# Output products of the late attention heads queued on TensorE behind a feed-forward product

## The chip, the cores and the metric

One core of a Trainium2 chip runs the whole program. The metric is the device time of one execution in microseconds (us). The kernel before was timed three times: 1084.61, 1088.86 and 1091.10 us, median 1088.86 us.

## The reference

```python
# q, k, v: (4, 8, 576, 64), f: (4, 8, 576); 32 heads in all, D = 64
scores = q @ k.T / sqrt(D);  cum = cumsum(log(clip(f, 1e-4, 1)))
scores = where(causal, -1e9, scores + cum[i] - cum[j])
attn   = softmax(scores);    attn_out = attn @ v
x = attn_out as (2304 tokens, 512)          # 4 batches x 576 tokens, 8 heads x 64
h = relu(x @ w1_in);   x = (h * h) @ w1_out          # first feed-forward, d_ff = 2048
h = x @ w2_in;         out = (h - tanh(h)) @ w2_out  # second feed-forward, d_ff = 2048
```

## The kernel before

All three parts run in one stream. Feed-forward operands are kept as a high and a low float32r part, and each product is the sum of three matmuls (high by high, low by high, high by low).

**Feed-forward.** The loop at the end of the kernel runs over steps g. Sixteen steps make a block of tokens (j, i = divmod(g, 16)). Blocks 0 to 7 are the first feed-forward, with 288 tokens each (block j needs the attention of batch j // 2). Blocks 8 to 12 are the second one. Step g calls `h_step` (L131), a product of 12 matmuls into the tile `hp`, then Relu and two Squares on ScalarE, which give `gh`, and a subtraction, which gives `gl` (on VectorE, except for the first two blocks). Two steps later (LAG = 2) `y_step` (L158) adds 12 matmuls into the tiles `yp`, 8 of them from `gh` and 4 from `gl`. `gh` and `gl` have three buffers each, and `hp` has one PSUM bank until block 6. Below, h 67 and y 67 are the products of step g = 67; the count starts at 0, so that 68 steps are done once y 67 is.

**Attention.** It runs beside blocks 0 to 5 as a generator, `chain()`, which hands out 196 pieces; `advance(to)` (L655) draws pieces up to a number given by `PACE`. It is called twice in a step, behind `h_step` and behind `y_step`. Pieces 116 to 195 are those of the late heads: five for each k from 17 to 32 (`attention_late`, L580). In the five pieces the scores of head k are made (`s_ps`, 12 matmuls), softened, turned by VectorE into the tile T (`turn`), and written to DRAM from T by one DMA (`put`, 1 MB), while the head before, k - 1, is finished: `split_p` splits its attention tile PTl into PTh (four instructions of POOL, L90) and a new PTl (four of VectorE, L101), and `pv` (L493) makes the output product, ten matmuls, of which those at L518 read PTh and PTl. Behind the fifth piece `get(k)` reads head k back from DRAM into PTl by four DMAs. PTl, PTh and T have one buffer each. So `get(k)` has to wait for `put(k)` and for `pv(k - 1)`, and `pv(k)` has to wait for `get(k)` and the split. With an odd head `pv` is followed by `store_x`, which writes a pair of heads to `x_d`; block 6 starts with a load of `x_d` (L705), which needs the last pair, heads 30 and 31.

**Order of the work.** Every engine runs its instructions in the order of its queue. For what is emitted before block 2 that order is the order of emission. Behind it a planner picks the order of each engine by its own simulated times. It is free to put `pv` ahead of feed-forward products that were emitted earlier, when by its times PTh and PTl are there. One rule limits it from the other side: `h_step` is queued behind the last TensorE instruction of an attention piece some pieces back (`SLK`: 8 in block 1, 3 in block 2, 8 in blocks 3 and 4, no rule in block 5).

By `PACE` the output products of heads 16 to 31 are emitted right behind these feed-forward products (head: product): 16: y 31; 17: y 34; 18: y 37; 19: y 40; 20: h 45; 21: y 49; 22: h 55; 23: y 56; 24: y 62; 25: y 67; 26: h 74; 27: h 79; 28: y 80; 29: y 83; 30: y 86; 31: y 89. For head 25, as an example: its `pv` lies in piece 116 + 5 x 9 + 4 = 165; in block 4 the pieces go from 160 to 177 over 32 half steps, and 160 + int(17 x 12 / 32) = 166 is reached in the second call of i = 5, that is in step 69, behind y 67.

Of the kernel before, what the change touches and what calls it, by code (L numbers as in the profile page):

```python
# [53 lines left out]
def kernel(  # L54
# [10 lines left out]
    nc = tc.nc  # L65
# [14 lines left out]
    def pre(u):  # L80
        return "" if u < UT else "l_"

    def by(name):
        return {"A": nc.scalar, "V": nc.vector, "P": nc.gpsimd, "S": nc.sync}[ENG[name]]

    def rounded(eng, out, in_):
        if eng is nc.scalar:
            eng.activation(out, in_, AF.Copy)  # L88
        elif eng is nc.gpsimd:
            eng.tensor_scalar(out, in_, 1.0, 1.0, ALU.mult, ALU.mult)  # L90
        else:
            eng.tensor_copy(out, in_)
# [114 lines left out]
    def load(u):  # L207
        R[u] = one.tile([128, 2, S], F32, tag="R", name="R")
        nc.sync.dma_start(R[u], qk[u])
        QB[u] = two.tile([68, 2, S], F32R, tag="QB", name="QB")  # L210
        nc.sync.dma_start(QB[u][64:68].bitcast(F32), aug_d[u])
# [7 lines left out]
    def prep(u):  # L219
        r = R.pop(u)  # L220
        qa = two.tile([128, 2, S], F32R, tag="QA", name="QA")
        QA[u] = qa
        split_qk(r, qa, QB[u], *(pre(u) + x for x in ("qb_q", "qa_lo", "qb_lo")))
        ST[u] = two.tile([128, 4, 6], F32, tag="ST", name="ST")
        by(pre(u) + "st").memset(ST[u], 1.0)

    def load_v(u):
        VR[u] = two.tile([128, 5, D], F32, tag="VR", bufs=2, name="VR")
        nc.sync.dma_start(VR[u], v[u])

    def prep_v(u):
        VH[u] = one.tile([128, 4, 2, D], F32R, tag="VH", name="VH")
        rounded(by(pre(u) + "vh"), VH[u][:, :, 0], VR[u][:, 0:4])
        rest(by(pre(u) + "vl"), VH[u][:, :, 1], VR[u][:, 0:4], VH[u][:, :, 0])
# [167 lines left out]
    def store_x(b, pair, xs, c0, c1):  # L402
        STORED.add((b, pair, c1))
        n = c1 - c0
        xh = one.tile([128, S], F32R, tag="xsh", name="xsh")
        rounded(by(pre(b * H) + "xh"), xh[:, :n], xs[:, c0:c1])
        rest(by(pre(b * H) + "xl"), xs[:, c0:c1], xs[:, c0:c1], xh[:, :n])
        nc.sync.dma_start(x_d[b][pair][:, 0, c0:c1], xh[:, :n].bitcast(F32))
        nc.sync.dma_start(x_d[b][pair][:, 1, c0:c1], xs[:, c0:c1])
# [21 lines left out]
    def bank(u, name):  # L431
        return psa.tile([128, 512], F32, tag="at", name=name)

    def scores(u, t):
        qa, qb, st = QA[u], QB[u], ST[u]
        n, q0 = NKEY[t], Q0[t]
        rows = 64 if t == 0 else 128
        cuts = [(0, 320), (320, 576)] if t == 4 else [(0, n)]
        mn = None
        for i, (a, b) in enumerate(cuts):  # L440
            ps = bank(u, "s_ps")
            nc.tensor.matmul(ps[:, :b - a], qa[:, 0, q0:q0 + 128], qa[:, 1, a:b], start=True, stop=False)  # L442
            nc.tensor.matmul(ps[:, :b - a], qb[:, 0, q0:q0 + 128], qb[:, 1, a:b], start=False, stop=True)  # L443
            mn = row_min(P[t], ps, st, t, i, a, b, mn)
        soften(P[t], st, t, mn, f"{pre(u)}n{t}")
# [20 lines left out]
    def turn(t):  # L466
        p, T = P[t], PT["t"]
        if t == 0:
            nc.vector.transpose(T[0:64, 0:2, 3, 0], p[0:64, :64].rearrange("p (b j) -> p b j", b=2))
            return  # L470
        nch = min(t + 1, 4)
        nc.vector.transpose(T[:, :, :nch, t - 1].rearrange("p b a j -> p a b j"),  # L472
                            p[:, :nch * 128].rearrange("p (a b j) -> p a b j", a=nch, b=4))
        if t == 4:
            nc.vector.transpose(T[:, 0:2, 2, 0], p[:, 512:576].rearrange("p (b j) -> p b j", b=2))

    def put(u):
        by("put").dma_start(p_d[u % 2], PT["t"].rearrange("p b a s j -> p (b a s j)"))
# [7 lines left out]
    def split_p(a):  # L486
        hi, lo = PT["h"], PT["l"]
        for c in (2 * a, 2 * a + 1):
            s0 = max(0, c - 1)
            rounded(by("pth"), hi[:, :, c, s0:], lo[:, :, c, s0:].bitcast(F32))  # L490
            rest(by(f"ptl{c}"), lo[:, :, c, s0:], lo[:, :, c, s0:].bitcast(F32), hi[:, :, c, s0:])

    def pv(u):  # L493
        vh, vr = VH.pop(u), VR.pop(u)
        b, h = divmod(u, H)
        e = h % 2
        ps = bank(u, "o_ps")
        if u < UT:
            hi, lo = (PT[k].rearrange("p q a s j -> p (q a s j)").rearrange("p (c t j) -> p c t j", c=4, t=4) for k in "hl")
            po = ps.rearrange("p (s j) -> p s j", s=4)  # L500
            at = lambda p, c, t: p[:, c, t:]
            po4, p4 = ps[0:64, 384:512].rearrange("p (q j) -> p q j", q=4), PT["t"][0:64, :, 3, 1]
            po_at = lambda t: po[:, t:]
            p0 = PT["t"][0:64, 2:4, 3, 0]
        else:
            hi, lo = PT["h"], PT["l"]
            po = ps.rearrange("p (q s j) -> p q s j", q=4, s=4)
            at = lambda p, c, t: p[:, :, c, t:]
            po4, p4 = po[0:64, :, 3], lo[0:64, :, 2, 0].bitcast(F32)
            po_at = lambda t: po[:, :, t:]  # L510
            p0 = lo[0:64, 0:2, 3, 0].bitcast(F32)
        seq = [(hi, 0), (hi, 1), (lo, 1), (hi, 2), (lo, 2), (hi, 3), (lo, 3), (None, 4), (lo, 0)]
        for n, (pt, c) in enumerate(seq):
            if pt is None:
                nc.tensor.matmul(po4, vr[0:64, 4], p4, start=False, stop=False)  # L515
                continue
            t = max(0, c - 1)
            nc.tensor.matmul(po_at(t), vh[:, c].rearrange("p a d -> p (a d)"), at(pt, c, t), start=(n == 0), stop=(n == 8))  # L518
        ps0 = bank(u, "o0_ps")
        nc.tensor.matmul(ps0[0:64, 0:64], vr[0:64, 0], p0, start=True, stop=True)  # L520
        if e == 0:
            XS[0] = two.tile([128, S], F32, tag="xs", name="xs")
        xs = XS[0]
        r = slice(64 * e, 64 * e + 64)
        xt = one.tile([64, 512], F32, tag="xsh", name="xt")
        rounded(nc.scalar, xt, ps[64:128])
        if u < UT:
            nc.vector.tensor_tensor(xs[r, 64:], ps[0:64], xt, ALU.add)
        else:
            nc.vector.tensor_tensor(  # L530
                xs[r, 64:].rearrange("p (s q j) -> p q s j", s=4, q=4),
                ps[0:64].rearrange("p (q s j) -> p q s j", q=4, s=4),
                xt.rearrange("p (q s j) -> p q s j", q=4, s=4), ALU.add,
            )
        rounded(by(pre(u) + "xs0"), xs[r, 0:64], ps0[0:64, 0:64])
        if e == 1:
            store_x(b, h // 2, xs, 0, S)
# [42 lines left out]
    def attention_late():  # L580
        for k in range(UT + 1, NU + 1):
            now = k < NU
            if now:
                load_v(k)
                scores(k, 4)
            yield
            if now:
                scores(k, 3)
                turn(4)
            yield  # L590
            if k + 1 < NU:
                prep(k + 1)
            prep_v(k - 1)
            split_p(0)
            if now:
                scores(k, 2)
                turn(3)
            yield
            if k + 2 < NU:
                load(k + 2)  # L600
            split_p(1)
            if now:
                scores(k, 1)
                scores(k, 0)
                turn(2)
            yield
            if now:
                turn(1)
                turn(0)
                put(k)  # L610
            pv(k - 1)
            yield
            if now:
                get(k)
# [26 lines left out]
    def chain():  # L641
        yield from first_b()
        steady_init()
        load(H)
        yield from attention(H)
        yield from attention_late()

    ga = chain()
    cnt = [0]
    PEI = {}  # L650
    NB_PIECES = 5 * H
# [1 line left out]
    total = A1 + 5 * (NU - UT)  # L653

    def advance(to):  # L655
        while cnt[0] < min(to, total):
            next(ga, None)
            PEI[cnt[0]] = next(x for x in reversed(nc.cur_bb.bb.instructions) if x.engine == EngineType.PE)
            cnt[0] += 1
# [78 lines left out]
    for g in range(len(BLK) * NF + LAG):  # L738
# [40 lines left out]
        if j < len(PACE):  # L779
            lo, hi, end = PACE[j]  # L780
            advance(lo + int((hi - lo) * min(1.0, (2 * i + 2) / end)))
# [60 lines left out]
```

## Time and profile before

| What | Value |
|---|---|
| Time of the profiled execution / its span | 1085.49 us / 1083.6 us |
| Median of three timed runs | 1088.86 us |
| TensorE matmul busy | 1026.8 us, 95% |
| TensorE weight load busy | 897.2 us, 83% |
| VectorE / ScalarE / GpSimd busy | 596.5 / 524.8 / 248.4 us |
| Mean granted TensorE clock | 0.987 |
| Chain that ended last | TensorE 58%, DMA 9%, VectorE 4% |

The span starts with attention and weight preparation. The late heads run from about 270 to 560 us beside blocks 2 to 5, the rest of the first feed-forward follows until about 675 us, and the second feed-forward fills the rest. In the profile PE is TensorE, PEld its weight loads, DVE is VectorE, ACT is ScalarE, POOL is GpSimd, and SP is the engine whose queue issues all DMAs here. PEclk is the granted clock as a share of 2.4 GHz; the trace knows two levels, 2.4 and 1.2 GHz.

### The profile page before, as it was taken

The numbers are of one execution on the slowest core, as the hardware profiler recorded it, in microseconds if no ns is written. First come the engines' busy times: TensorE is split into PE (matmuls) and PEld (weight loads), VectorE is DVE, ScalarE is ACT, GpSimd is POOL, SyncE is SP. The second block draws the span as 40 slices with busy tenths as digits, with TensorE's granted clock in tenths as the row PEclk, the third lists the DMA queues.
The fourth block names the chain that finished last, engine by engine and source line by source line (L and its number), as shares of the span: only waits on it lengthen the run. The fifth ranks groups of instructions, "written<-read, shape, count | busy, mean of one in ns | idle before, by whom it ended". The sixth has DMA issues, their size and how long they took to land.

```text
span 1083.6 us, 16842 instructions
## 1 busy us (share of the span) xinstructions
PE 1026.8 (95%) x6048; PEld 897.2 (83%) x6048; DVE 596.5 (55%) x1599; ACT 524.8 (48%) x1221; POOL 248.4 (23%) x357
## 2 busy tenths in 40 slices
PE   3889999999999898999989999999999999999998
PEld 3577678888998788988989999888888888888898
DVE  7897767777787777877524546542222222222232
ACT  5987777765555546454526657432222222222232
POOL 4243455564453442533210000000000000000000
PEclk9999999999999999999989999999999999999999
DMA  6565643225955648845546088100200300110010
GB/s 207 222 167 179 196 145 120 90 84 172 294 170 179 205 146 259 257 141 162 169 148 253 2 281 306 45 1 8 109 1 1 117 1 1 39 39 1 1 40 21
DMA packets 63301, 134.83 MB, mean 124 GB/s; under 512 B 6416, under 2 KB 31568, under 8 KB 61168
## 3 DMA queue, kind: packets, MB, share of 16 engines
q1 hardware_dynamic: 63216, 133.74, 38.7%
q8 instruction: 48, 0.79, 0.3%
q14 instruction: 37, 0.30, 0.1%
HBM read 93.94 MB, written 39.78 MB: 123 GB/s over the span
## 4 chain that ended last, share of the span: by engine, by line
PE 58%; DMA 9%; DVE 4%; POOL 1%; SPq 1%; ACT 1%; issue 1%; POOLq 0%; DVEq 0%
PE yp L164 28%; PE hp L138 27%; DMA PTl<-p_d 6%; DMA p_d<-T 3%; PE o_ps L518 2%; DVE PTl L101 2%; SPq L484 1%; POOL PTh L90 1%; DVE gl L101 1%; DVE T L472 1%; DVE QA L101 0%; PE s_ps L442 0%; PE s_ps L443 0%; PE o_ps L515 0%; ACT P L425 0%
## 5 line engine op out<-in xcount | busy, mean ns | idle before, releaser
L138 PE MATMUL hp<-xhl,w 128*128 128x288 f32 (+2 forms) x2496 | 451.4, 328 | 3.9 <-ACT tmp L148 2.2
L138 PEld LDWEIGHTS hp<-xhl,w 128*128 128x128 f32 x2496 | 386.0, 190 | 42.4 <-ACT tmp L148 3.7
L164 PE MATMUL yp<-ghl,w 128*128 128x512 f32 (+1 forms) x960 | 216.0, 374 | 0.0
L164 PE MATMUL yp<-gh,w 128*128 128x288 f32 x1024 | 200.3, 301 | 0.1
L164 PEld LDWEIGHTS yp<-ghl,w 128*128 128x128 f32 x960 | 168.4, 188 | 34.5
L153 DVE TENSOR_TENSOR tmp<-hp,tmp 128x512 f32<-128x512 f32 (+1 forms) x80 | 51.0, 638 | 209.9 <-ACT tmp L152 209.9
L164 PEld LDWEIGHTS yp<-gh,w 128*128 128x128 f32 x1024 | 162.0, 192 | 2.6 <-issue 1.1
L152 ACT ACTIVATE tmp<-hp 128x512 f32<-128x512 f32 (+1 forms) x80 | 44.4, 555 | 225.0 <-PE hp L138 224.9
L164 PE MATMUL yp<-gl,w 128*128 128x288 f32 x512 | 135.2, 303 | 3.6 <-DVE gl L101 2.8
L148 ACT ACTIVATE tmp<-hp 128x288 f32<-128x288 f32 x128 | 51.8, 406 | 115.2 <-PE hp L138 112.1
L425 ACT ACTIVATE P<-P,ST 128x320 f32<-128x320 f32 (+4 forms) x151 | 84.6, 562 | 38.5 <-DVE ST L416 38.1
L164 PEld LDWEIGHTS yp<-gl,w 128*128 128x128 f32 x512 | 91.3, 192 | 6.4 <-DVE gl L101 3.9
L101 DVE TENSOR_TENSOR ghl<-tmp,ghl 128x512 fp32r<-128x512 f32 (+1 forms) x80 | 51.1, 638 | 49.1 <-ACT ghl L88 49.1
L429 POOL TENSOR_SCALAR P<-P,ST 128x448 f32<-128x448 f32 (+4 forms) x88 | 55.9, 636 | 96.3 <-DVE ST L428 53.7
L416 DVE CUSTOM_DVE_ANT_0 P<-s_ps,mk 128x320 f32<-128x320 f32 (+3 forms) x151 | 63.8, 432 | 21.7 <-PE s_ps L443 14.4
L101 DVE TENSOR_TENSOR gl<-tmp,gh 128x288 fp32r<-128x288 f32 x96 | 47.7, 498 | 49.7 <-ACT tmp L150 49.2
L88 ACT ACTIVATE ghl<-tmp 128x512 fp32r<-128x512 f32 (+1 forms) x80 | 47.2, 590 | 49.9 <-DVE tmp L153 49.8
L101 DVE TENSOR_TENSOR PTl<-PTl,PTh 128x512 fp32r<-128x512 f32 (+1 forms) x64 | 51.9, 840 | 35.2 <-POOL PTh L90 35.1
L101 DVE TENSOR_TENSOR w<-wst,w 128x512 fp32r<-128x512 f32 x64 | 45.6, 719 | 28.1 <-ACT w L88 28.0
L90 POOL TENSOR_SCALAR PTh<-PTl 128x512 fp32r<-128x512 f32 (+1 forms) x64 | 46.4, 750 | 56.9 <-DMA PTl<-p_d 56.3
L149 ACT ACTIVATE gh<-tmp 128x288 fp32r<-128x288 f32 x128 | 56.5, 443 | 4.1 <-PE yp L164 1.2
L150 ACT ACTIVATE tmp<-tmp 128x288 f32<-128x288 f32 x128 | 56.1, 439 | 2.2
(120 smaller groups left out, 1194.6 us busy)
## 6 DMA issues: line engine op xcount, KB each, us to landing
raw<-in_w_dram SPq DMA_DIRECT2D x64, 512.0 KB
p_d<-T SPq DMA_DIRECT2D x16, 1024.0 KB
PTl<-p_d SPq DMA_DIRECT2D x64, 256.0 KB
R<-in_qk_dram SPq DMA_DIRECT2D x24, 576.0 KB
xhl<-y_d SPq DMA_DIRECT2D x16, 512.0 KB
xhl<-x_d SPq DMA_DIRECT2D x14, 576.0 KB
y_d<-yst SPq DMA_DIRECT2D x14, 576.0 KB
VR<-in_v_dram SPq DMA_DIRECT2D x32, 160.0 KB
```

The lines of the kernel that those rows point to most:

```text
L88: eng.activation(out, in_, AF.Copy)
L90: eng.tensor_scalar(out, in_, 1.0, 1.0, ALU.mult, ALU.mult)
L101: eng.tensor_tensor(out, in_, hi.bitcast(F32), ALU.subtract)
L138: nc.tensor.matmul(ps, w[:, k * 128:(k + 1) * 128], xk, start=(jj == 0), stop=(jj == 11))
L148: nc.scalar.activation(tmp, ps, AF.Relu)
L149: nc.scalar.activation(gh, tmp, AF.Square)
L150: nc.scalar.activation(tmp, tmp, AF.Square)
L153: nc.vector.tensor_tensor(tmp, ps, tmp, ALU.subtract)
L164: nc.tensor.matmul(yp[m][:, :n], w[:, c], x, start=(i == 0 and j == 0), stop=(i == NF - 1 and j == 2))
L416: nc.vector.tensor_tensor_reduce(p[:rows, a:b], ps[:rows, :b - a], mk[:rows, o:o + b - a], -0.125, 3.0e38 if mn is None else mn, ALU.add, ...
L425: nc.scalar.activation(p[:rows, :n], p[:rows, :n], AF.Exp, bias=mn, scale=-1.0, accum_out=st[:rows, 1, t:t + 1])
L429: by(n_by).tensor_scalar(p[:rows, :n], p[:rows, :n], st[:rows, 3, t:t + 1], 1.0, ALU.mult, ALU.mult)
```

## The change

`advance` notes the TensorE instruction that was emitted last before it draws pieces, which is the last matmul of an `h_step` or a `y_step`, in `FF[0]`. In `attention_late` the call of `pv(k - 1)` is wrapped in `tc.issue_after(FF[0])`: each TensorE instruction that `pv` emits gets an edge that puts it behind that matmul in TensorE's queue. The edge is on the order of the queue alone; there is no semaphore and no wait for the matmul to end. What `pv` puts on the other engines has no such edge. The planner plans again with these edges.

```diff
@@ attention_late @@
                 turn(1)
                 turn(0)
                 put(k)
-            pv(k - 1)
+            with tc.issue_after(FF[0]):
+                pv(k - 1)
             yield
             if now:
                 get(k)
@@
     ga = chain()
+    FF = [None]
     cnt = [0]
     PEI = {}
@@
     def advance(to):
+        FF[0] = next(x for x in reversed(nc.cur_bb.bb.instructions) if x.engine == EngineType.PE)
         while cnt[0] < min(to, total):
             next(ga, None)
```

## Rows read from the trace of the kernel before

**Rows 1.** The page, busy time, share of the span, instructions:
```profile
PE 1026.8 (95%) x6048; PEld 897.2 (83%) x6048; DVE 596.5 (55%) x1599; ACT 524.8 (48%) x1221; POOL 248.4 (23%) x357
```

**Rows 2.** Waits of TensorE, 270 to 560 us: total us, times, longest:
```profile
PE o_ps L518 <- POOL PTh L90: 15.5, 8, 4.2
PE yp L164 <- DVE gl L101: 2.8, 2, 1.5
```

**Rows 3.** Sums by stretch, feed-forward alone: busy us (instructions) by engine, PEclk, DMA, GB/s:
```profile
560.00:675.00 115.00, 115.00 (x862) 114.78 (x861) 56.40 (x112) 72.77 (x164) 0.00 (x0) 1.00 0.62 220
```

**Rows 4.** Timeline of TensorE, first product of heads 21, 25, 27, 29, 31:
```profile
358.34 0.50 PE L518 MATMUL o_ps<-PTh,VH 128*128 128x512 f32 x1 [3.59 <-POOL PTh L90]
...
433.91 0.50 PE L518 MATMUL o_ps<-PTh,VH 128*128 128x512 f32 x1 [1.58 <-POOL PTh L90]
...
471.79 0.49 PE L518 MATMUL o_ps<-PTh,VH 128*128 128x512 f32 x1 [1.10 <-POOL PTh L90]
...
509.55 0.69 PE L518 MATMUL o_ps<-PTh,VH 128*128 128x512 f32 x1 [1.85 <-POOL PTh L90]
...
546.09 0.80 PE L518 MATMUL o_ps<-PTh,VH 128*128 128x512 f32 x1 [4.21 <-POOL PTh L90]
```

**Rows 5.** Sums by stretch around three of these products:
```profile
430.00:440.00 10.00, 8.42 (x49) 7.77 (x49) 8.59 (x21) 4.38 (x13) 5.73 (x6) 0.83 0.77 220
505.00:515.00 10.00, 8.15 (x47) 7.33 (x47) 7.71 (x27) 3.58 (x13) 3.76 (x6) 0.83 0.59 168
546.00:552.00 6.00, 5.91 (x26) 5.24 (x27) 3.68 (x7) 1.30 (x3) 2.33 (x4) 0.61 0.01 3
```

**Rows 6.** L164 (y products) up to the first product of heads 21, 25, 27, 29, 31:
```profile
0.00:358.33 358.33, 96.28 (x585) 84.11 (x585) 0.99 0.56 173
...
0.00:433.90 433.90, 126.63 (x772) 111.59 (x772) 0.98 0.57 177
...
0.00:471.78 471.78, 143.40 (x876) 126.89 (x876) 0.98 0.58 180
...
0.00:509.54 509.54, 156.48 (x964) 139.06 (x964) 0.98 0.58 180
...
0.00:546.08 546.08, 171.11 (x1056) 152.46 (x1056) 0.98 0.58 178
```

**Rows 7.** L138 (h products) up to the first product of heads 27 and 31:
```profile
0.00:471.78 471.78, 141.75 (x888) 126.78 (x888) 0.98 0.58 180
...
0.00:546.08 546.08, 168.69 (x1068) 151.84 (x1068) 0.98 0.58 178
```

**Rows 8.** Timeline around head 21, ScalarE, then VectorE:
```profile
353.75 0.43 ACT L150 ACTIVATE tmp<-tmp 128x288 f32<-128x288 f32 x1
...
358.32 1.09 DVE L101 TENSOR_TENSOR PTl<-PTl,PTh 128x512 fp32r<-128x512 f32 x1 [4.86 <-POOL PTh L90]
...
362.02 0.91 DVE L101 TENSOR_TENSOR gl<-tmp,gh 128x288 fp32r<-128x288 f32 x1
```

**Rows 9.** Timeline of TensorE, last product of heads 27, 28, 29, 31:
```profile
477.85 0.50 PE L518 MATMUL o_ps<-PTl,VH 128*128 128x512 f32 x1
...
500.47 0.50 PE L518 MATMUL o_ps<-PTl,VH 128*128 128x512 f32 x1
...
517.32 0.50 PE L518 MATMUL o_ps<-PTl,VH 128*128 128x512 f32 x1
...
553.53 0.50 PE L518 MATMUL o_ps<-PTl,VH 128*128 128x512 f32 x1
```

**Rows 10.** Timeline of SP: put and get of head 28, load of block 6:
```profile
480.67 0.33 SPq L478 DMA_DIRECT2D p_d<-T  x1
...
485.67 1.75 SPq L484 DMA_DIRECT2D PTl<-p_d  x4
...
558.25 1.95 SPq L705 DMA_DIRECT2D xhl<-x_d  x2
```

**Rows 11.** Timeline of TensorE, h 95 and the start of block 6:
```profile
568.24 3.76 PE L138 MATMUL hp<-xhl,w 128*128 128x288 f32 x27
```

## The prediction

> **What bounds the kernel now.** I read the page first: TensorE holds a matmul for 95% of the span [rows 1], so the end is moved only by what lets TensorE stand still or slows it. The waits of TensorE in the stretch of the late heads come second. One line carries most of them: the first output product of a head, which waits for PTh from POOL, 15.5 us in eight waits; the y products wait for `gl` 2.8 us in two [rows 2]. The sums by stretch come third. With feed-forward alone TensorE is never idle, and 862 matmuls take 115.0 us [rows 3], 133.4 ns each, 1.60 us for a product of twelve; I price every h and y product with that. The timeline comes fourth: heads 21, 25, 27, 29 and 31 begin with an idle TensorE, 3.59, 1.58, 1.10, 1.85 and 4.21 us [rows 4], 12.3 of the 15.5 us. What the reader is to see: TensorE has work left (feed-forward), and it stands behind an instruction that isn't ready. PTh needs a round trip through DRAM, and the planner's order expects it sooner than it comes.
>
> There is a second cost. Behind the waits of heads 25, 29 and 31 the granted clock falls to 0.83, 0.83 and 0.61 of the stretch [rows 5]. With two levels, 2.4 and 1.2 GHz, the work lost is (1 - 0.83) x 10 = 1.7 us, again 1.7, and (1 - 0.61) x 6 = 2.3, in sum 5.7 us. Without the wait I expect no fall: with TensorE kept busy it is granted in full [rows 3].
>
> **Which heads move.** The edge matters only where `pv` now runs ahead of its named product. The matmuls counted up to the first product say where each stands. Head 25 starts with 772 / 12 = 64.3 y products done, and needs 68 (y 67). Head 29 starts with 80.3 and needs 84, head 31 with 88 and needs 90, head 21 with 48.75 and needs 50 [rows 6]. Head 27 starts with 888 / 12 = 74 h products and needs 80 (h 79) [rows 7]. So each of these gets feed-forward put ahead of it that runs where TensorE now waits, from 2.0 us at head 21 (1.25 products) to 9.6 us of h products alone at head 27. Heads 24, 26, 28 and 30 stand ahead of their products too, by one to three, but none of them begins with such a wait. Heads 16 to 20, 22 and 23 already stand behind theirs, and I leave their 3.2 us of waits (15.5 - 12.3) as they are.
>
> **The sum.**
> 1. Waits of heads 25, 27, 29 and 31: 1.58 + 1.10 + 1.85 + 4.21 = 8.7 us gone. That the feed-forward ahead of them covers the wait is clear for 25, 27 and 29 (3.7 x 1.60 = 5.9 us at the least against under 2); for head 31 it is h 89, y 88 and y 89, 4.8 us against 4.21. Head 21 I count at nothing (bounds a loss of 2.4 and a gain of 3.6), for a reason that is rival A.
> 2. Clock behind them: 5.7 us gone (bounds 0 and 5.7).
> 3. Waits of y products for `gl`, which now end last more often. The trace shows two, 2.8 us [rows 2], over some eight heads that stand about where the edge wants them: 0.35 us a head, and nine heads move: 3.2 us added (bounds 0 and nine of the longest, 1.5 each, 13.5).
> 4. The end of attention. `get(k)` waits for `pv(k - 1)`, so a later `pv` makes the next head's four DMAs later, and with them what stands behind them in SP's queue (loads of heads, stores of x). Head 27 moves most. It has 6 h products [rows 7] and at least 4 y products (876 / 12 = 73 now [rows 6], 77 wanted, since `gh` has three buffers) to let pass, 16.0 us, less 4.4 saved at heads 25 and 27: its first product comes at 471.8 + 16.0 - 4.4 = 483.4 [rows 4]. It now runs until 478.35 [rows 9], 6.6 us; so it ends at 490.0. Four heads are then left. From the end of head 28 (500.97 [rows 9]) to the first product of head 29 (509.55 [rows 4]) are 8.6 us; with a run of 6.6 a head takes 15.2 (bounds: 10.6, with a run of ten matmuls in a row, about 2.0; and 18.9, the mean of the last four now, (554.03 - 478.35) / 4 [rows 9]). Head 31 then ends at 490.0 + 60.8 = 550.8. Block 6 needs its x. The load's issue now ends 6.2 us behind head 31 (560.2 [rows 10]) and block 6 starts 15.8 behind it, at 568.24 + 1.60 [rows 11]; its need lies between, I take 11: 561.8. By then TensorE must have run dry to lose anything. Now at 546.08 it has 96 - 89 h [rows 7] and 96 - 88 y products [rows 6] of blocks up to 5 left, 15 x 1.60 = 24.0, with head 31 (2.0) and the slow clock (2.3) until 574.4; less the gain of items 1 to 3 (11.2) that is 563.2. The x is there 1.4 us earlier: nothing lost (bounds 0, and at 18.9 us a head 490.0 + 75.6 + 11 - 563.2 = 13.4).
>
> Gain: 8.7 + 5.7 - 3.2 = 11.2 us. The profiled execution took 1085.5, which gives 1074.3. The median of the timed runs lies 3.4 higher, and so I forecast 1077.7, rounded to 1078. Its own range, by half of the clock loss staying or two or three us of item 4 coming true, is 1074 to 1085.
>
> **Rivals.**
>
> A, no difference: the wait moves from `pv` to the y product. VectorE is in order too. At head 21 `gl` of step 49 was ready to be subtracted at 354.2, when ScalarE had ended its square, and was subtracted at 362.02, behind a PTl subtraction that waited for POOL until 358.32 [rows 8]. y 49 needs it, and the change puts `pv(21)` behind y 49: its first product would come behind 362.9 + 0.5 = 363.4 instead of 358.3. In between TensorE has eight `gh` matmuls (1.1 us) and one h product (1.6) to do, 2.7 of 5.1 us; 2.4 us are lost there. If VectorE's order is the same at the other four heads, the idle time stands in front of y products instead of in front of `pv`, about as long, and the clock falls as now; what one head loses another gives back, within 2.4 us either way: 1085.5, on the median 1089. For it: the rows just named [rows 8]. Against it: at heads 25, 27 and 29 the feed-forward ahead is 5.9 us and more, and what keeps VectorE waiting there is no longer than the wait of TensorE, under 2 us; one h product and eight `gh` matmuls alone cover that.
> The Trainium skill ("TensorE: Matmul & The Clock Gate", section "Architectural detail: the array is 16× 32×32, not 1× 128×128") states that VectorE and ScalarE are strict first-in, first-out. The trace agrees (7.8 us between the square and the subtraction); by that rule alone, with VectorE's order kept, rival A would be the forecast.
>
> B, slower: the chain of the last heads becomes the bound. Head 27 ends some 12 us later than now, and what was saved is lost in front of block 6 if the last four heads take over 18.35 us each (490.0 + 4 x 18.35 + 11 = 574.4, that is 563.2 + 11.2). At 19.7, the mean of head 28 (500.97 - 478.35 = 22.6) and head 29 (517.82 - 500.97 = 16.85 [rows 9]), the loss is 16.6 against 11.2: 1090.9, on the median 1094. For it: their mean is 18.9 now, already past the point. Against it: head 28 is long since its `get` at 485.67 waited for its `put` at 480.67 [rows 10], which comes behind the end of head 27; `put` doesn't need `pv`, and with `pv` held back it can be done before it, so that only the 8.6 us and the run are left.
>
> C, more: head 21 gains its 3.6 us as well and no wait for `gl` is added: 14.4 + 3.6 = 18.0, 1067.5, on the median 1071. That asks that the planner also moves the `gl` subtractions ahead of the split.
>
> That the change does nothing is excluded by rows 6 and 7, unless the planner's new order differs in some other way; this is part of A.
>
> **How the numbers follow.** Forecast 0.44, A 0.22, B 0.24, C 0.10. Of the forecast 0.40 lies over 0.5% below the median (0.5%, 5.4 us, is about what a measurement of this kernel can tell from no change) and 0.04 within. Faster 0.40 + 0.10 = 0.50; same 0.22 + 0.04 = 0.26; slower 0.24. The range reaches from below C (1068) to above B's price (1096), which leaves B's longer cycles and better luck than C out.
>
> **What would show it.** Step 1: heads 25, 27, 29 and 31 begin without a wait for POOL, with the counts of rows 6 and 7 at 68, 80, 84 and 90 or more. Step 2: the granted clock stays at 1.00 there. Step 3: the waits of L164 for `gl` stay under 6 us; if they come to 10 or more, it is A. Step 4: block 6 starts without an idle TensorE; if it waits there for the load of x, or if the late heads again begin with waits, it is B. The forecast is wrong if the late heads' waits are gone and the span is not shorter.

## The result, and the profile after

The changed kernel takes 1098.4 us (median of 5 runs, 1095.8 to 1100.5) against 1088.9 of the kernel before: 1.0089 times as long, 95% interval 1.0066 to 1.0112. It is slower; 1077.7 was forecast.

The page of the profiled execution (1100.47 us, span 1098.7), where [rows 1] stood:

```profile
PE 1030.4 (94%) x6048; PEld 901.5 (82%) x6048; DVE 595.2 (54%) x1599; ACT 525.8 (48%) x1221; POOL 249.9 (23%) x357
```

The same 6048 matmuls hold TensorE 3.6 us longer, and it is idle for 1098.7 - 1030.4 = 68.3 us, where it was 56.8: 3.6 + 11.5 make up the 15.1 us by which the span grew. The waits of TensorE in the late heads, 270 to 600 us, say where the idle time went (compare [rows 2]; us in total, count, longest; `ST` holds the small row sums of the softmax, `yst` takes a finished y out of `yp`, and `yp` is free for the next block only then):

```profile
PE o_ps L518 <- POOL PTh L90: 11.5, 6, 3.5
PE yp L164 <- DVE ST L427: 7.2, 2, 5.6
PE yp L164 <- DVE gl L101: 6.8, 3, 5.4
PE hp L138 <- ACT tmp L148: 3.7, 3, 2.2
PE yp L164 <- DVE yst L101: 2.6, 1, 2.6
PE hp L138 <- DMA xhl<-x_d: 1.1, 1, 1.1
```

The waits for POOL fell by 4.0 us only, and waits of feed-forward products for VectorE and ScalarE came in their place: 7.2 + 6.8 + 3.7 + 2.6 = 20.3 us against 2.8 for `gl` before and 0.9 in two smaller lines of the same kind. The two largest, from the timeline of TensorE:

```profile
363.05 1.33 PE L164 MATMUL yp<-gl,w 128*128 128x288 f32 x4 [5.39 <-DVE gl L101]
364.17 0.63 PE L518 MATMUL o_ps<-PTh,VH 128*128 128x512 f32 x1
...
446.32 1.33 PE L164 MATMUL yp<-gl,w 128*128 128x288 f32 x4 [5.64 <-DVE ST L427]
```

The first is at head 21: y 49, and right behind it the head's first output product. The second is y 65, ahead of head 25 (788 matmuls of L164 came before it: 65 products of twelve, and eight of y 65). Both are the four `gl` matmuls of a y product. What VectorE did ahead of the second, with ScalarE's last square of that step first:

```profile
438.94 0.43 ACT L150 ACTIVATE tmp<-tmp 128x288 f32<-128x288 f32 x1
...
439.37 2.00 DVE L101 TENSOR_TENSOR PTl<-PTl,PTh 128x512 fp32r<-128x512 f32 x2 [3.37 <-POOL PTh L90]
...
441.76 2.45 DVE L101 TENSOR_TENSOR PTl<-PTl,PTh 128x384 fp32r<-128x384 f32 x2
...
444.78 0.76 DVE L101 TENSOR_TENSOR QA<-R,QA 64x576 fp32r<-64x576 f32 x1
...
445.64 0.62 DVE L101 TENSOR_TENSOR gl<-tmp,gh 128x288 fp32r<-128x288 f32 x1
```

The operands of `gl` were there at 439.4. VectorE had stood for 3.37 us in front of the first PTl subtraction until POOL delivered PTh, and `gl` stands behind all four of these and what lies between them: it is done at 446.3. The standing itself ended as the operands came; it had made the split late, and the 6.9 us from there are VectorE's work in the order of its queue. (The view names the instruction behind it, ST, as the releaser; `gl` is what y 65 reads. The other 1.6 us of the ST line and the 2.6 of yst stand at 520.7 and 516.8: there the first products of a new block wait until VectorE, with the next head's split in its queue, has emptied `yp`.) The source of the delay is the trip through DRAM, issue by SP and start of POOL:

```profile
430.42 1.75 SPq L484 DMA_DIRECT2D PTl<-p_d  x4
...
438.72 2.12 POOL L90 TENSOR_SCALAR PTh<-PTl 128x512 fp32r<-128x512 f32 x3 [7.43 <-DMA PTl<-p_d]
```

TensorE had run out of other work at 440.7. The first part of PTh was there by then, so the first output product of head 25, which in the kernel before started at 433.91 [rows 4], could have started here too; but its place in the queue was now behind y 67, and it ran at 455.15. The matmuls counted up to the first product of heads 21, 25, 29 and 31 (L164) and of head 27 (L138) show that the edge does what it says (before: [rows 6, 7]): 50, 68, 85.6 and 92 y products where at least 50, 68, 84 and 90 were asked for, and 80 h products where 80 were.

```profile
0.00:364.10 364.10, 97.29 (x600) 85.27 (x600) 0.99 0.55 171
0.00:455.10 455.10, 132.48 (x816) 117.38 (x816) 0.97 0.57 176
...
0.00:539.80 539.80, 166.41 (x1027) 147.83 (x1027) 0.97 0.56 172
0.00:571.50 571.50, 178.67 (x1104) 158.76 (x1104) 0.97 0.55 170
...
0.00:503.50 503.50, 156.02 (x960) 140.42 (x960) 0.97 0.55 171
```

The granted clock falls behind the new waits, as it did behind the old ones [rows 5]; sums by stretch:

```profile
363.00:373.00 10.00, 9.95 (x38) 8.52 (x39) 5.83 (x16) 3.06 (x7) 4.03 (x5) 0.55 0.60 210
446.00:452.00 6.00, 5.68 (x29) 5.68 (x30) 4.17 (x18) 1.91 (x5) 0.59 (x2) 0.63 0.47 180
```

The end of attention: last product of head 27, first and last of head 31, and the first of block 6 (compare [rows 4, 9, 11]):

```profile
505.32 0.50 PE L518 MATMUL o_ps<-PTl,VH 128*128 128x512 f32 x1
...
571.55 0.50 PE L518 MATMUL o_ps<-PTh,VH 128*128 128x512 f32 x1 [2.64 <-POOL PTh L90]
...
578.29 0.50 PE L518 MATMUL o_ps<-PTl,VH 128*128 128x512 f32 x1
...
588.11 2.10 PE L138 MATMUL hp<-xhl,w 128*128 128x288 f32 x14 [1.07 <-DMA xhl<-x_d]
```

From head 29 to block 6 TensorE waits 1.74 us for PTh at head 30, 2.64 at head 31 and 1.07 for x, 5.45 in sum. In the kernel before it was 1.85 + 4.21 = 6.06 us at heads 29 and 31 [rows 4], and nothing in front of block 6. Attention ends about 25 us later than before, and the chain at its end adds no idle time.

### The profile page after: what moved, and what is told of

It reads as the page before. It is cut to its first block, busy times and chain, and to the rows that moved or that the text cites. A ratio compares the mean times of both kernels' runs of the same rounds, so it can differ in the third digit from the quotient of the medians.

```text
span 1098.7 us, 16850 instructions
## 1 busy us (share of the span) xinstructions
PE 1030.4 (94%) x6048; PEld 901.5 (82%) x6048; DVE 595.2 (54%) x1599; ACT 525.8 (48%) x1221; POOL 249.9 (23%) x357
## 4 chain that ended last, share of the span: by engine, by line
PE 66%; DMA 14%; DVE 9%; ACT 3%; issue 3%; POOL 3%; SPq 2%; POOLq 0%; ACTq 0%; DVEq 0%
PE yp L164 28%; PE hp L138 28%; DMA PTl<-p_d 7%; DMA p_d<-T 3%; DVE PTl L101 2%; PE o_ps L518 2%; PE o_ps L344 2%; DMA raw<-in_w_dram 2%; SPq L484 1%; POOL PTh L90 1%; DVE P L416 1%; PE s_ps L442 1%; DMA R<-in_qk_dram 1%; PE s_ps L443 1%; PE t_ps L453 1%
## 5 line engine op out<-in xcount | busy, mean ns | idle before, releaser
L138 PE MATMUL hp<-xhl,w 128*128 128x288 f32 (+2 forms) x2496 | 455.0, 329 | 7.5 <-ACT tmp L148 4.9
L138 PEld LDWEIGHTS hp<-xhl,w 128*128 128x128 f32 x2496 | 388.9, 192 | 46.2 <-ACT tmp L148 6.1
L164 PE MATMUL yp<-ghl,w 128*128 128x512 f32 (+1 forms) x960 | 216.0, 374 | 0.0
L164 PE MATMUL yp<-gh,w 128*128 128x288 f32 x1024 | 200.2, 301 | 4.2 <-DVE yst L101 2.6
L164 PEld LDWEIGHTS yp<-ghl,w 128*128 128x128 f32 x960 | 168.4, 188 | 34.5
L164 PEld LDWEIGHTS yp<-gh,w 128*128 128x128 f32 x1024 | 161.9, 192 | 6.9 <-DVE yst L101 2.7
L164 PE MATMUL yp<-gl,w 128*128 128x288 f32 x512 | 133.3, 302 | 12.7 <-DVE gl L101 6.8
L164 PEld LDWEIGHTS yp<-gl,w 128*128 128x128 f32 x512 | 90.5, 191 | 15.0 <-DVE gl L101 13.6
L429 POOL TENSOR_SCALAR P<-P,ST 128x448 f32<-128x448 f32 (+4 forms) x88 | 60.6, 690 | 98.2 <-DVE ST L428 53.4
```

The lines of the kernel that those rows point to most:

```text
L138: nc.tensor.matmul(ps, w[:, k * 128:(k + 1) * 128], xk, start=(jj == 0), stop=(jj == 11))
L164: nc.tensor.matmul(yp[m][:, :n], w[:, c], x, start=(i == 0 and j == 0), stop=(i == NF - 1 and j == 2))
L429: by(n_by).tensor_scalar(p[:rows, :n], p[:rows, :n], st[:rows, 3, t:t + 1], 1.0, ALU.mult, ALU.mult)
```

## The experiments

Two theories were put up. V: the loss is VectorE's queue, in which `gl` stands behind a PTl subtraction that waits for DRAM, while `pv`, the work that could fill the gap, is held back. C: the loss is the chain from head to head, which a later `pv` lengthens until the last heads and block 6 come late. Single profiles of one program differ by a few us in the launch and in single waits, so verdicts rest on the ratios. Where lines were added to a kernel, its line numbers are one higher (L519 for L518).

**Where the loss is: heads 16 to 23, 24 to 31.**
```diff
-            with tc.issue_after(FF[0]):
+            with tc.issue_after(FF[0]) if k - 1 < 24 else ExitStack():     # in the other run: k - 1 >= 24
```


> The edge only for heads 16 to 23, so that of the heads that move only head 21 does. Theory V: head 21's wait becomes one for gl of about 5.4 us instead of 3.6 for the split, with its slow clock; 2 to 4 us over before, 1091 to 1093. Theory C: nothing is held back far enough to matter, within 1 us of before, 1088 to 1090.

Measured 1.0012 of before (0.9982 to 1.0042), which can't be told from no change. The wait at head 21 did turn from one for the split into one for `gl` (350 to 425 us; the second line is head 23):
```profile
PE yp L164 <- DVE gl L101: 5.6, 1, 5.6
PE o_ps L518 <- POOL PTh L90: 3.4, 1, 3.4
```
V had the wait right (5.4 expected). Its price, 2 to 4 us, and C's, within 1 us, both lie in the interval.

> The edge only for heads 24 to 31. Theory V: head 21 waits 3.6 us for the split as before; one wait for gl of about 5 us at head 25 and smaller ones for VectorE behind it; 1093 to 1096. Theory C: the whole loss is here, 1097 to 1100, and the end of head 31 comes as late as in the changed kernel (about 20 us or more behind that of before).

Measured 1.0089 (1.0061 to 1.0118), 1097.9 us: the loss lies with heads 24 to 31. The time is C's, and so is the end of attention: the last product of head 31 starts at 576.3 us, 22.8 behind the kernel before (553.53 [rows 9]). The waits are V's (TensorE, 425 to 530 us, 12.6 us in these lines and one of 0.4), and block 6 waits 1.2 us for x.
```profile
PE yp L164 <- DVE ST L427: 4.6, 2, 3.0
PE yp L164 <- DVE gl L101: 2.7, 2, 2.0
PE hp L138 <- ACT tmp L148: 2.5, 2, 2.1
PE yp L164 <- DVE yst L101: 2.4, 1, 2.4
```

**The second half split again: heads 24 to 27, 28 to 31, 31 alone.** The edits are as above, with `24 <= k - 1 < 28`, `k - 1 >= 28` and `k - 1 == 31`.

> The edge only for heads 24 to 27, whose feed-forward products lie furthest behind. Both halves of the last run's loss are told apart: theory V puts all of it here (waits behind a held-back VectorE at heads 25 to 28): 1096 to 1100. Theory C puts it at the end, where heads 28 to 31 come late whether or not they have the edge: also 1096 to 1100, but then with idle TensorE from head 29 to block 6 of 8 us and more, against under 5 by V.

Measured 1.0058 (1.0035 to 1.0081), 1098.1 us, the time that both expected. TensorE's waits for `gl`, ScalarE and yst between 425 and 530 us are 5.4 + 3.1 + 1.1 = 9.6 us. From head 29 to block 6 the waits are one of 2.1 us at head 30 and one of 1.3 for x, under 5 as V had it, though head 31 has no edge here and ends as late as in the run before (575.9). Not all of the 9.6 us is loss, since the waits for PTh in the same stretch, 4.5 us before, are gone.

> The edge only for heads 28 to 31. Theory V: no gl stands far behind here, and the waits of 1.85 and 4.21 us at heads 29 and 31 with their slow clock shrink: 0 to 5 us below before, 1083 to 1088. Theory C: delaying these heads delays block 6 directly, 1092 to 1097 with a wait for the load of x in front of it.

Measured 0.9963 (0.9946 to 0.9981): faster than before. V's sign and size, and against C, since block 6 waits for the last two of these heads. In the profile that wait is 0.4 us (500 to 600 us).
```profile
PE o_ps L518 <- POOL PTh L90: 4.8, 2, 3.2
PE hp L138 <- DMA xhl<-x_d: 0.4, 1, 0.4
PE yp L164 <- DVE gl L101: 0.2, 1, 0.2
```

> The edge only for head 31, the one with the longest wait (4.21 us and 2.3 us of slow clock). Theory V: h 89 is run in front of it, but y 88 and y 89 need a gl behind the split, so at most half of the 6.5 us is won: 0 to 3 us below before. Theory C: block 6 waits for x by what head 31 is later, within 1 us of before or up to 3 us over it.

Measured 1.0009 (0.9983 to 1.0036): the time tells neither theory from the other. The profile shows rival A at its plainest. Head 31 begins without a wait, and in place of its 4.21 us [rows 4] a y product ahead of it waits 4.36 us for a `gl` that stands behind three PTl subtractions:
```profile
551.00 2.66 DVE L101 TENSOR_TENSOR PTl<-PTl,PTh 128x512 fp32r<-128x512 f32 x3 [6.83 <-POOL PTh L90]
553.58 0.45 DVE L101 TENSOR_TENSOR gl<-tmp,gh 128x288 fp32r<-128x288 f32 x1
...
554.09 1.33 PE L164 MATMUL yp<-gl,w 128*128 128x288 f32 x4 [4.36 <-DVE gl L101]
```
The sum of the parts (0.1 + 0.6 - 0.4%) falls short of the whole (0.9%). The planner lays out everything behind an edge anew, which may be why, and was not tested; the intervals leave part of the gap to noise. So each part is read by its own waits.

**VectorE's order, first try: the split behind the `gl` emitted last.**
```diff
-            split_p(0)
+            with tc.issue_after(GL[0]):        # GL[0]: the gl subtraction emitted last
+                split_p(0)
...                                             # the same for split_p(1)
```


> Changed kernel, and besides the VectorE subtractions of the split (PTl) are queued behind the gl subtraction of the feed-forward step emitted last. Theory V (VectorE's order: the y products that now have to run ahead of pv need a gl that stands behind a PTl subtraction, which waits for the trip through DRAM): the waits of 5.4 us at head 21 and 5.6 us at head 25 fall under 1 us each, waits of y products for VectorE between 340 and 530 us fall from about 16 us to under 5, time 1080 to 1089. Theory C (the chain of heads: a later pv makes each later get later, and the last heads come too late): the split comes still later, so nothing is gained, 1097 to 1105, with waits at heads 30 and 31 and in front of block 6 as long as now (5.5 us in sum) or longer.

Measured 1.0120 (1.0046 to 1.0194; four runs only), 1099.9 us: V's time is missed. The two waits of over 5 us are gone, but shorter ones stand in their place: y products wait for VectorE 9.7 us from 340 to 530 us, the longest 2.5, where V expected under 5 and the changed kernel has 16.6. In its profile TensorE is idle 4.9 us less than in the changed kernel and busy 3.4 longer, and the time hardly follows, so this run is no support for V's price. As I read the code, its edge is too weak: `split_p` is emitted one or two pieces ahead of `pv`, and the y products that `pv` is put behind belong to later steps, whose `gl` still stands behind the split.

**The split's subtractions on POOL.**
```diff
-    "ptl0": "V", "ptl1": "V", "ptl2": "V", "ptl3": "V",
+    "ptl0": "P", "ptl1": "P", "ptl2": "P", "ptl3": "P",
```


> Changed kernel, with the PTl subtractions of all late heads on POOL instead of VectorE, so that VectorE never waits for the trip through DRAM. Theory V: waits of y products for gl in the late heads go under 2 us in sum, and so does the wait for yst; the split takes some 3 us more a head; time 1085 to 1093. Theory C: the longer split lengthens the chain by about 3 us a head, 1100 to 1115, idle TensorE ahead of the last heads and of block 6.

Measured 1.0070 (1.0034 to 1.0105), 1093.9 us: 0.9 us above V's range and well under C's. But 5.2 us of waits for `gl` remain between 425 and 530 us where V expected under 2, and C's sign is there: TensorE waits 6.0 us for x in front of block 6. The wait for VectorE's `gl` has moved one engine on. POOL, then VectorE:
```profile
485.41 2.25 POOL L90 TENSOR_SCALAR PTh<-PTl 128x512 fp32r<-128x512 f32 x4 [7.39 <-DMA PTl<-p_d]
487.63 4.71 POOL L101 TENSOR_TENSOR PTl<-PTl,PTh 128x512 fp32r<-128x512 f32 x4
492.33 0.64 POOL L429 TENSOR_SCALAR P<-P,ST 128x448 f32<-128x448 f32 x1
...
493.00 0.71 DVE L472 STREAM_TRANSPOSE T<-P 128x512 f32<-128x512 f32 x1 [4.49 <-POOL P L429]
```
The scaling of P now stands behind the split in POOL's queue, VectorE's `turn` waits for it, and `gl` for VectorE. V as "VectorE waits for DRAM" is too narrow: here it is POOL that stands in front of the split for 7.39 us and holds what is queued behind it.

**VectorE's order, second try: the split in the piece of `pv`.**
```diff
-            split_p(0)      # third piece
...
-            split_p(1)      # fourth piece
...
+            with tc.issue_after(GL[0]):
+                split_p(0)
+                split_p(1)
             with tc.issue_after(FF[0]):
                 pv(k - 1)
```


> Changed kernel, with the whole split of a late head emitted in the same piece as its pv, and its VectorE part queued behind the gl subtraction of the step emitted last. Now no gl that a feed-forward product ahead of pv needs can stand behind a PTl subtraction that waits for DRAM. Theory V: the waits of TensorE for gl, for ScalarE and for yst between heads 24 and 28 fall from 13.7 us to under 5; the split's own 4 us before each pv are covered by feed-forward or not, so 1082 to 1092. If instead holding back pv is costly by itself (theory C, a longer chain from head to head), the split's delay adds to it: 1098 to 1110, with idle TensorE ahead of the last heads and of block 6 above 8 us.

Measured 1.0032 (1.0009 to 1.0055), 1093.2 us, 1 us over V's range. The waits behind VectorE go (1.5 us for `gl` is all that is left from 425 to 530 us), and part of what C says comes true at the end, 500 to 600 us:
```profile
PE o_ps L519 <- POOL PTh L90: 6.6, 3, 3.2
PE hp L138 <- DMA xhl<-x_d: 4.1, 1, 4.1
```
Block 6 waits 4.1 us. So the same edit was made where the loss lies, at heads 24 to 27, with the edge there and without it.

> Heads 24 to 27 alone have the edge, as in the run before, and heads 24 to 27 alone have their split emitted with pv, its VectorE part behind the gl emitted last. Theory V (held gl): TensorE's waits for gl, ScalarE and yst between heads 24 and 28 fall from about 7 us to under 3, and the 0.6% over before fall to within 0.3% of before, 1085 to 1092. If holding pv back costs by the chain (theory C): 1.005 to 1.010 of before, as the edge alone, with the idle time at heads 28 to 31 and block 6.

Measured 0.9975 (0.9950 to 1.0001), 1085.8 us. With the edge alone on heads 24 to 27 it was 1.0058; the intervals don't meet. TensorE, 425 to 530 us, all lines:
```profile
PE o_ps L519 <- POOL PTh L90: 6.2, 3, 2.5
PE hp L138 <- ACT tmp L148: 0.2, 1, 0.2
```
The 9.6 us of waits behind VectorE and ScalarE are 0.2, and 6.2 us of waits for PTh have come back, 6.4 in sum against 10.4 with the edge alone. Head 31 is still late (its last product starts at 567.0, 13.5 us behind the kernel before), and the time is no longer than before: against C. How much of the 0.8% between the two runs is the edge's cost, and how much the late split wins by itself, takes a run without the edge. The late split does one thing more: VectorE doesn't stand in front of it, and its four subtractions take 2.09 us, where they took 4.45 in the changed kernel at head 25.
```profile
430.19 2.09 DVE L101 TENSOR_TENSOR PTl<-PTl,PTh 128x512 fp32r<-128x512 f32 x4
```

> The control: no edge at all, but the split of heads 24 to 27 emitted with pv, its VectorE part behind the gl emitted last. The split comes later, so pv does too, and the planner sees that. Theory V: VectorE holds no gl back and the planner fills TensorE by its own order: within 0.3% of before. Theory C: like the edge, since these heads become late all the same: 1.004 to 1.010 of before.

Measured 0.9956 (0.9931 to 0.9981), 1084.1 us: better than V expected, and against C. So 0.4% is the late split's own gain. With the late split the edge costs 0.9975 / 0.9956 = 1.002, which the intervals don't tell from nothing; without it 1.0058. The drop is about as large as what the intervals leave open. What carries V's reading is the drop together with the waits: at these heads most of what the edge cost went by way of VectorE's queue. That it costs nothing else is not shown.

> The edge for heads 28 to 31, which measured 0.996 of before, and the late split for heads 24 to 27 without the edge. If the late split frees VectorE at no cost (theory V), 0.993 to 0.998 of before; if it makes the heads late (theory C), the gain of the edge is lost, 1.000 to 1.006, with a wait in front of block 6.

Measured 0.9961 (0.9937 to 0.9984), 1083.0 us: as without the edge, so the two gains (0.4% each) don't add. Block 6 waits 2.0 us. Both versions beat the kernel before and the changed one.

> No edge; the late split for heads 20 to 27 instead of 24 to 27 (which measured 0.9956 of before). Theory V: the waits at heads 20, 21, 23 and for gl ahead of heads 22 and 24, about 10 us with their slow clock, shrink by a third to a half: 0.989 to 0.996 of before. Theory C: heads 20 to 23 are made late for nothing and with them all that follow: 0.996 to 1.003, with a longer wait in front of block 6 than the 2.7 us of the run with heads 24 to 27.

Measured 0.9988 (0.9962 to 1.0015): C's outcome, with 3.6 us in front of block 6. The late split pays for four heads; for eight no gain can be told.

## Why the prediction was wrong

**What bounds, which heads move: right.** TensorE's idle time set the end, the heads named moved, and no first product of heads 25, 27 and 29 waits for POOL any more. (Head 26 stood four h products ahead of its place, not three at the most: 852 matmuls of L138 up to 456.79 us, 71 products, where h 74 asks for 75.)

**Item 1, the waits that go: half.** Of the 8.7 us at the four heads 6.1 went (head 31 still waits 2.64), and the 3.6 at head 21. But heads 23 (3.5 us) and 30 (1.7), which waited 0.8 or not at all, now do, so that of 15.5 us in all only 4.0 went.

**Item 2, the clock: the wrong way.** The falls moved with the waits. Behind the 5.39 us at head 21 the clock is at 0.55 for ten us, 4.5 us of work lost where 5.7 in sum were to be won.

**Item 3, waits for `gl`: the step that failed.** I added 3.2 us with a bound of 13.5, from waits in an order in which `pv` was free to fill the gaps. The waits for VectorE and ScalarE grew by 20.3 - 3.7 = 16.6 us: for `gl` alone from 3.0 to 12.4, three times the term, and 7.2 more for ScalarE's `tmp` and for `yp` at the start of a block, which were in no term. By the sign of step 3 (10 us and more for `gl`) this is rival A, but not at rival A's price of no difference. I had its mechanism, and worked out within a us when head 21 would start behind y 49 (363.4; 364.17 measured), but argued that one head's loss is another's gain and that a wait of under 2 us would be covered at heads 25 to 29. That took VectorE's wait for as long as TensorE's. What counts is the time from the moment a `gl` could be made to the moment it is: at head 25 that was 6.9 us, with the whole split in it that had stood until then, and meanwhile TensorE was forbidden the one thing that was ready.

**Item 4 and rival B, the chain: not the cause.** Head 27 starts at 503.59, not at 483.4, and ends at 505.8, not at 490.0; between 270 us and its start the waits for VectorE and ScalarE are 15.5 us, where they were 2.8, and the slow clock at head 21 takes 4.5. The last four heads take (578.79 - 505.82) / 4 = 18.2 us each, not 15.2; and block 6 waits 1.07 us. Rival B had the sign and, at 1094, came nearest to the time, 4 us short. That was luck, for the idle time from head 29 to block 6 didn't grow (5.45 us against 6.06), the edge on the last four heads alone is a gain, and with the later split at heads 24 to 27 an end of attention 13.5 us later went with no loss of time. How the late split of all or of eight heads loses at the end of attention was seen (4.1 and 3.6 us in front of block 6) and not taken apart.

## What to carry to other kernels

An edge that holds work back on one engine's queue takes that work out of the gaps it was filling; before it is set, follow what must now run first back through the queues of the other engines, and count from when each operand could be made to when it is. Where a planner expects a transfer too early, try to hold back the instructions that wait for the transfer on the shared queues (here VectorE's part of the split) and not only their last consumer. Here that paid over four heads (0.9956), and over eight no gain could be told.

## What the runs showed of the hardware

The lower clock outlasts the wait by far. TensorE was busy for 9.95 of the ten us from 363 to 373 and was granted 0.55 in the mean, by the two levels nine us at 1.2 GHz; behind the longest wait of the late heads before it was 0.61 over six us, 4.7 of them at 1.2 GHz [rows 5].

The trip through DRAM takes 8.3 us from the first issue of a `get` to the start of POOL (430.42 to 438.72), of which the four issues take 1.75.

The same PTl subtraction has two speeds. The four of a late head take 2.09 us on VectorE when they run once all of PTh is there, and at head 25 of the changed kernel, where POOL was still writing PTh beside the first two, 2.00 for two and 2.45 for the other two. Whether POOL's work beside it is the reason was not tested.
